# Softmax denominators folded with two half-width matmuls, a single transpose for the inverses, and moved pieces, in a routed attention followed by an MLP

## The chip, the core and the metric

The kernel runs on one core of a Trainium2 chip. The metric is the device time of one execution in microseconds (us); lower is better. A kernel is an instruction list for each of five engines: TensorE (PE in the profile, with its weight loads as PEld), VectorE (DVE), ScalarE (ACT), GpSimd (POOL) and SyncE (SP, which issues most transfers). Each list runs in the order in which the program emitted it; lists wait for one another by semaphores. A tile of PSUM is a bank, and a bank that is to be used again waits for its last readers.

## What is computed

The attention has 4 batches, 8 heads, 768 tokens and a head dimension of 64. Each query and key is assigned to the nearest of 16 centroids of its head, and a query attends only to keys of its own cluster. The result, seen as 3072 rows of 512, goes through a two-layer MLP with a PReLU.

```python
q_assign = np.argmax(np.einsum('bhsd,hcd->bhsc', q_n, c_n), axis=-1)
k_assign = np.argmax(np.einsum('bhsd,hcd->bhsc', k_n, c_n), axis=-1)
mask = q_assign[:, :, :, None] == k_assign[:, :, None, :]
scores = np.where(mask, scale * np.matmul(q, k.transpose(0, 1, 3, 2)), -1e9)
attn = np.exp(scores - np.max(scores, axis=-1, keepdims=True))
attn = attn / (np.sum(attn, axis=-1, keepdims=True) + 1e-09)
x = heads_to_columns(np.matmul(attn, v))          # 3072 x 512
h = x @ w_in                                      # 512 -> 2048
return (np.maximum(h, 0.0) + alpha * np.minimum(h, 0.0)) @ w_out
```

## The kernel before

**Units of work.** A pair n is two heads of a batch; there are 16. Pairs 0 to 11 (batches 0 to 2) are done in halves of 384 queries. For a half, all 6 chunks of 128 keys are scored against the queries (score, L712, with keys on the partitions), exponentiated by ACT, masked by DVE (mask, L761: E times "cluster of the query equals cluster of the key"; batch 0 gets its mask from a bf16 matmul, L740, instead), and multiplied by v on PE (weigh, L838). Pairs 12 to 15 (batch 3) are sorted by cluster beforehand, through a scratch in DRAM, so that a chunk of keys meets only the chunks of queries beside it. There the two halves are called sides, the product is weigh_near (L884), normalised results go to rows by PE transposes (to_rows, L923), are scattered by POOL (put_back, L933), and are read back and turned by DVE (fetch_back, L940).

**Denominators.** DVE adds the chunks of E (add_up L776, add_near L785), turns the sum in blocks of 32 by 32 (turn, L798) and reduces it (rows_sums, L805) to "part" of 128 x 24, 12 columns for each of the two heads. total (L813) folds it over the partitions by a matmul with a 0/1 matrix. invert (L821) takes reciprocals from PSUM, spreads them with one transpose for each head (64 partitions each, L832), and calls check (L326), which takes the smallest and largest bit pattern of the inverses by two reductions. normalise (L961) multiplies. The first half of batch 0 gets its denominators from PE (weigh with denominators, L854) instead. total, prep_sims, prep_clusters, order_sims, order_begins, one side of weigh_near and to_rows all take the one mps bank that misc (L84) hands out.

**MLP pieces.** While one batch half is attended, the MLP of the half before is fed in pieces (ffn_pieces, L972). hidden(f) makes block f of 16: four matmuls (eight PE records, since a float32 matmul is two records) into one of two fps banks that are used in turn, a copy gT by ACT, and the PReLU slope on gT by DVE in place (slopes, L978). Slopes of a block are emitted in the next hidden; where f % 4 is 3, directly after the copy (L997). final(i, f0) multiplies four blocks with w_out for 128 rows, again eight records, and when its sum over blocks is complete, ACT copies it to y or DVE adds it to y (L1015). For the first half of batch 0 the order is four hiddens, three finals, four hiddens, and so on; for all others eight hiddens, six finals, twice. Pieces also force the conversion of the float64 weights they need (convert, L242: split and join on DVE, scale on ACT, a product on POOL, L269).

**Order.** Everything is emitted by hand. There are 84 steps u, three to a pair's half (or sorted pair); s is a step's place among its three. Steps 0 to 11 attend the first half of batch 0, steps 12 to 23 its second. In these a step scores two chunks, weighs the two before, adds (from step 12), and in s = 2 turns and reduces; then come three slots with the pieces of the MLP and the preparations of later pairs, and total at the end of s = 2. Steps 12 to 23 are fed 3, 2, 2, 2, 2, 2, 3, 2, 2, 2, 2, 2 pieces: where it is two, they stand in the second and third slot. Thus hiddens 0 to 2 are in step 12, hidden 3 and the first final in 13, hiddens 4 and 5 in 15, 6 and 7 in 16, and the first final over blocks 4 to 7 in 17; hiddens 10 and 11 are in 19 and their first final in 20; hidden 15 and its final are in 23. A conversion that splits in a slot joins six slots later. From step 24 on a half or sorted pair scores three chunks, inverts and weighs the pair before, scores the other three, and spreads the DVE work (todo) over 12 slots: s = 0 has two of them, s = 1 and s = 2 five each. later (L95) puts a piece so many slots ahead; prep_at names a step and a slot; load_at a step. At the end the remaining pieces are fed at every second tick (L1228).

**Names that follow.** every is the bf16 image of all clusters of a pair (L433), copied by ACT from the mps bank of prep_clusters; order_counts (L553) finds the clusters of a pair that is to be sorted and counts them; order_blocks (L670) turns the sorted q and k; order_constants (L488) builds constants for the sort before step 25.

Of the kernel before, what the change touches and what calls it, by code (L numbers as in the profile page):

```python
# [10 lines left out]
FP32 = mybir.dt.float32  # L11
# [3 lines left out]
I32 = mybir.dt.int32  # L15
# [8 lines left out]
def kernel(  # L24
# [122 lines left out]
    alf = const.tile([NF, P], FP32, name="alf")  # L147
# [10 lines left out]
    fold = const.tile([P, P], FP32, name="fold")  # L158
    spread = const.tile([P, P // Q, P], BF16, name="spread")
    nc.gpsimd.memset(spread, 0.0)  # L160
    for g in range(P // Q):
        r = slice(g * Q, (g + 1) * Q)
        nc.gpsimd.tensor_copy(
            out=fold[r, :].rearrange("p (a i) -> p a i", i=Q),
            in_=ident[r, None, r].broadcast_to((Q, P // Q, Q)))
        nc.gpsimd.tensor_copy(out=spread[r, g, :], in_=fold[r, :])

# [34 lines left out]
    cn = const.tile([P, D], FP32, name="cn")  # L202
# [119 lines left out]
    lowest = const.tile([P, 2 * NP], FP32, name="lowest")  # L322
    highest = const.tile([P, 2 * NP], FP32, name="highest")
    WORDS = [float((127 + e) * 2 ** 23) for e in (-50, 40)]

    def check(n, half, inverses):  # L326
        i = 2 * n + half
        for to, op in ((lowest, ALU.min), (highest, ALU.max)):
            nc.vector.tensor_reduce(out=to[:, i:i + 1], in_=inverses.bitcast(I32), axis=AX.X,
                                    op=op)  # L330
# [157 lines left out]
    def order_constants():  # L488
        ordc = sorts["ordc"]
        stage = [ordc.tile([P, NX // PARTS, P], FP32, name=f"stage{i}") for i in range(STAGES)]  # L490
        for t in stage:
            nc.gpsimd.memset(t, 0.0)
        place = ordc.tile([P, HS], U16, name="place")
        nc.gpsimd.iota(place, pattern=[[1, HS]], base=0, channel_multiplier=0)

        number = ordc.tile([P, NX], I32, name="number")
        nc.gpsimd.iota(number, pattern=[[TS, NX]], base=0, channel_multiplier=1)

        kinds = [[[0, P // NC], [1, NC]], [[2, 2], [0, 2], [1, 2], [0, NC]],
                 [[0, 2], [1, 2], [0, Q]]]  # L500
        rows, cols = [], ordc.tile([P, 3], FP32, name="cols")
        brief = asg.tile([P, HS], FP32, name="simT")
        for i, pattern in enumerate(kinds):
            row = (ordc.tile([P, P], FP32, name=f"row{i}") if i else brief[:, 0:P])
            nc.gpsimd.iota(row, pattern=pattern, base=0, channel_multiplier=0,
                           allow_small_or_imprecise_dtypes=True)
            own = brief[:, P:2 * P]
            nc.gpsimd.tensor_tensor(out=own, in0=row, in1=ident, op=ALU.mult)
            nc.vector.tensor_reduce(out=cols[:, i:i + 1], in_=own, axis=AX.X, op=ALU.add)
            rows.append(row)  # L510
        same = brief[:, 2 * P:3 * P]
        nc.vector.tensor_scalar(out=same, in0=rows[1], scalar1=cols[:, 1:2], scalar2=None,
                                op0=ALU.is_equal)


        before, within = rows[1], rows[2]
        nc.vector.scalar_tensor_tensor(out=before, in0=rows[0], scalar=cols[:, 0:1],
                                       in1=same, op0=ALU.is_gt, op1=ALU.mult)
        nc.vector.scalar_tensor_tensor(out=same, in0=rows[0], scalar=cols[:, 0:1],
                                       in1=same, op0=ALU.is_equal, op1=ALU.mult)  # L520
        nc.vector.scalar_tensor_tensor(out=within, in0=rows[2], scalar=cols[:, 2:3],
                                       in1=same, op0=ALU.is_gt, op1=ALU.mult)
        nc.vector.tensor_tensor(out=within, in0=within, in1=before, op=ALU.add)


        shift = ordc.tile([P, 2], FP32, name="shift")
        nc.vector.tensor_scalar(out=shift[:, 0:1], in0=cols[:, 2:3], scalar1=-float(HS),
                                scalar2=None, op0=ALU.mult)
        nc.vector.tensor_scalar(out=shift[:, 1:2], in0=cols[:, 1:2], scalar1=2.0,
                                scalar2=float(S), op0=ALU.is_ge, op1=ALU.mult)  # L530
        nc.vector.tensor_scalar(out=shift[:, 1:2], in0=shift[:, 1:2], scalar1=-1.0,
                                scalar2=None, op0=ALU.add)
        begins = ordc.tile([P, NP - NO], FP32, name="begins")
        sorts.update(stage=stage, number=number, place=place, before=before, within=within,
                     shift=shift, begins=begins)
# [17 lines left out]
    def order_counts(n, ps):  # L553

        top, first, pieces = argmax(ps, exact=True)
        member = sorts["ordp"].tile([P, HS], BF16, name="mine")
        pieces.append(lambda: nc.vector.transpose(
            out=member, in_=top.rearrange("p t c -> p (t c)")))

        def scan():  # L560
            count = asg.tile([P, HS], FP32, name="simT")
            nc.vector.tensor_tensor_scan(count, member, member, 0.0, ALU.add, ALU.max)
            us[n] = member, count
        pieces.append(scan)
        for i, piece in enumerate(pieces):
            later(i, piece) if i else piece()
# [238 lines left out]
    def rows_sums(n, half):  # L805
        part = rdp.tile([P, 2 * NX], FP32, name="part")
        nc.vector.tensor_reduce(out=part, in_=accTs.pop((n, half)), axis=AX.X, op=ALU.add)
        parts[n, half] = part
# [4 lines left out]
    def total(n, half):  # L813

        if (n, half) in parts:
            ps = misc()
            nc.tensor.matmul(out=ps[:, 0:2 * NX], lhsT=fold, rhs=parts.pop((n, half)),
                             start=True, stop=True)
            totals[n, half] = ps

    def invert(n, half):  # L821

        if (n, half) not in totals:
            return
        ps = totals.pop((n, half))
        inv = rdp.tile([P, 2 * NX], FP32, name="inv")
        nc.vector.reciprocal(out=inv, in_=ps[:, 0:2 * NX])
        pool = sorts["ordp"] if n >= NO and half else rdp
        rd = pool.tile([P, HS], FP32, name="rd")
        for h in range(2):  # L830
            r = slice(h * D, (h + 1) * D)
            nc.vector.transpose(  # L832
                out=rd[r, :],
                in_=inv[r, h * NX:(h + 1) * NX, None].broadcast_to((D, NX, Q)))
        rds[n, half] = rd
        check(n, half, inv)

    def weigh(m, denominators=False):  # L838
# [24 lines left out]
        if denominators and done:  # L863
# [6 lines left out]
            inv = rdp.tile([P, 2 * NX], FP32, name="inv")  # L870
# [5 lines left out]
            for h in range(2):  # L876
                nc.vector.tensor_copy(out=inv[h * D + Q:(h + 1) * D, 0:NX],
                                      in_=inv[h * D:h * D + Q, 0:NX])
            rd = rdp.tile([P, HS], FP32, name="rd")
            nc.vector.transpose(out=rd, in_=inv[:, 0:NX, None].broadcast_to((P, NX, Q)))  # L880
            rds[n, half] = rd
            later(1, lambda: check(n, half, inv[:, 0:NX]))
# [17 lines left out]
    def normalise_near(n):  # L900
# [13 lines left out]

        starts = (4, 6) if n == NP - 1 else (6, 10)
# [7 lines left out]
    def to_rows(outT, rows, i):  # L923

        ps = misc()
        for j in range(HJ):
            nc.tensor.transpose(out=ps[:, j * P:(j + 1) * P],
                                in_=outT[:, (i * HJ + j) * P:(i * HJ + j + 1) * P],
                                identity=ident)
        later(1, lambda: nc.scalar.copy(  # L930
            rows[:, i * HJ:(i + 1) * HJ].rearrange("p j d -> p (j d)"), ps[:, 0:HS]))
# [40 lines left out]
    def ffn_pieces(b, half):  # L972
# [12 lines left out]
        def hidden(f):  # L985
# [11 lines left out]
            if f % FQ == FQ - 1:  # L997
                slopes()

        def final(i, f0, on, off):  # L1000
# [3 lines left out]
            unfinished[0] = not off  # L1004
            ps = pss[i]
# [41 lines left out]
    for (n, half), u in start_of.items():  # L1047
        def at(step, slot, piece):
            prep_at.setdefault((step, slot), []).append(piece)
        if half is None:  # L1050
# [7 lines left out]
            at(u - 4, FIRST, lambda n=n: prep_clusters(n))  # L1058
            for i in range(2):
                at(u - 2, FIRST + i, lambda n=n, i=i: order_blocks(n, i))  # L1060
                at(u - 1, FIRST + i, lambda n=n, i=i: order_queries(n, i))
            continue
        if half == 0:
# [16 lines left out]
            if n >= NCH:  # L1080
                at(u - 4, FIRST, lambda n=n: prep_clusters(n))
# [19 lines left out]
    def kept(block):  # L1101


        return {NS // UB - 2: 4, NS // UB - 1: 10}.get(block, 0)
# [52 lines left out]
    for u in range(TOGETHER, NS + 1):  # L1157
# [4 lines left out]
        if s == 0 or u == NS:  # L1162
# [6 lines left out]
            if prior[1] is None:  # L1169
                invert(prior[0], 1)  # L1170
# [21 lines left out]
            if half is None:  # L1192
# [4 lines left out]
                         lambda n=n: (total(n, 0), turn(n, 1), rows_sums(n, 1)),  # L1197
                         lambda n=n: invert(n, 0)]
                todo += [lambda: None] * 3 + [lambda n=n: total(n, 1)]
# [33 lines left out]
    good = const.tile([P, 2], FP32, name="good")  # L1233
    nc.vector.tensor_reduce(out=good[:, 0:1], in_=highest, axis=AX.X, op=ALU.max)
# [212 lines left out]
```

## Time and profile before

Three executions took 1002.57, 1004.88 and 1003.51 us, median 1003.51; the profiled one took 1003.53 with a span of 1001.4. TensorE's granted clock was full but for 7 us in all before 85 us.

| stretch, us | what | PE busy | DVE busy | POOL busy |
|---|---|---|---|---|
| 84.0 to 204.9 | batch 0, second half; MLP of the first | 119.8 of 120.9 | 94.5 | 26.1 |
| 204.9 to 302 | batch 1, with order_constants | 93.6 of 97.1 | 75.6 | 2.2 |
| 302 to 634 | batches 1 and 2 | 330.9 of 332.0 | 256.5 | 92.3 |
| 680.5 to 708.9 | pair 12 | 28.4 of 28.4 | 23.0 | 0 |
| 708.9 to 737.0 | pair 13 | 24.8 of 28.1 | 26.5 | 10.5 |
| 737.0 to 765.7 | pair 14 | 25.4 of 28.7 | 21.3 | 12.9 |
| 765.7 to 791.7 | pair 15 | 26.0 of 26.0 | 20.2 | 8.9 |
| 791.7 to 824.0 | end of pair 15, rows back | 30.1 of 32.3 | 7.3 | 16.4 |
| 824.0 to 1001.4 | MLP of batch 3 alone | 171.6 of 177.4 | 29.3 | 0 |

The table is the profile's busy time of each engine in each stretch. Busy time of PE contains the modelled end of each matmul: a hidden's record is busy 0.49 us, and the next one starts 0.32 us after it. A final's records start 0.43 us apart. In the page's groups, a line gives engine, operation, output and inputs, shape and count, then busy time in all and the mean of one in ns, then the idle time of the engine before such instructions and what ended it. In the timeline a line is one run of equal instructions: start, length, and in brackets the idle time before it with its releaser.

### The profile page before, as it was taken

Reading aid. Unit: us, or ns where it says so; the run is one execution under the profiler, and the core shown is the slowest. Engines: PE = TensorE matmul, PEld = TensorE weight load, DVE = VectorE, ACT = ScalarE, POOL = GpSimd, SP = SyncE. Lnnn points to the kernel's source line nnn. Section 1 sums busy time; section 2 is a strip of 40 time slices with the busy share of each in tenths; the row PEclk is TensorE's granted clock in tenths of the full one; section 3 lists DMA queues with packets and bytes.
Section 4 is the critical chain, followed back from the end, with each engine's and each line's share of the span. In section 5 each row is a group of like instructions: output and inputs, shape, how many; then the busy total and the mean of one; then the engine's idle time right before and its main releaser. Section 6 shows DMA issues by size and latency. Waiting matters only on the chain.

```text
span 1001.4 us, 10929 instructions
## 1 busy us (share of the span) xinstructions
PE 968.5 (97%) x3955; PEld 482.1 (48%) x3955; DVE 650.4 (65%) x1209; ACT 259.6 (26%) x468; POOL 211.8 (21%) x249
## 2 busy tenths in 40 slices
PE   8899999989999999999999999999988999999997
PEld 5434444445454454545445454454544545455453
DVE  5887788598487776877868698687987523021010
ACT  5655443223122221312222022231222101110110
POOL 2323222000000644301000263620044540000000
PEclk9989999999999999999999999999999999999999
DMA  6533553032100252415010121710521020000000
GB/s 248 199 108 108 137 135 71 16 67 44 32 1 21 87 114 56 84 40 106 1 32 0 53 80 34 148 35 17 85 60 31 24 50 22 0 5 29 0 1 34
DMA packets 174286, 60.46 MB, mean 60 GB/s; under 512 B 161216, under 2 KB 164752, under 8 KB 174224
## 3 DMA queue, kind: packets, MB, share of 16 engines
q1 hardware_dynamic: 168768, 51.42, 21.7%
q0 software_dynamic: 4608, 7.87, 2.3%
q8 instruction: 33, 0.54, 0.2%
q10 hardware_dynamic: 848, 0.39, 0.2%
q14 instruction: 29, 0.24, 0.1%
HBM read 45.15 MB, written 14.16 MB: 59 GB/s over the span
## 4 chain that ended last, share of the span: by engine, by line
PE 87%; DVE 8%; ACT 2%; issue 1%; DMA 1%; ACTq 0%; POOL 0%; DVEq 0%; POOLq 0%
PE fps L1007 31%; PE fps L989 31%; PE vps L861 8%; PE sps L731 7%; PE fps L731 3%; PE sps L740 1%; PE vps L897 1%; PE mps L371 1%; DVE gT L981 1%; DVE more L772 1%; PE mps L897 1%; DVE acc L801 1%; ACT E L752 1%; ACT member L416 1%; DMA aq<-member 1%
## 5 line engine op out<-in xcount | busy, mean ns | idle before, releaser
L989 PE MATMUL fps<-xT,w_in_sb 128*128 128x384 f32 x1024 | 342.9, 490 | 1.8 <-DVE y L1015 1.8
L1007 PE MATMUL fps<-w_out_sb,gT 128*128 128x512 f32 x768 | 339.2, 596 | 2.1 <-DVE gT L981 1.1
L989 PEld LDWEIGHTS fps<-xT,w_in_sb 128*128 128x128 f32 x1024 | 190.8, 190 | 140.5 <-issue 5.2
L1007 PEld LDWEIGHTS fps<-w_out_sb,gT 128*128 128x128 f32 x768 | 143.5, 190 | 173.9 <-issue 162.1
L637 POOL DMA_INDIRECT scratch<-stage,off x96 | 101.7, 1059 | 333.9 <-DMA stage<-in_v_dram 275.3
L981 DVE SCALAR_TENSOR_TENSOR gT<-gT,alpha 128x384 f32<-128x384 f32 x128 | 80.5, 635 | 133.8 <-ACT gT L995 127.1
L995 ACT COPY gT<-fps 128x384 f32<-128x384 f32 x128 | 61.3, 479 | 337.3 <-PE fps L989 328.4
L731 PE MATMUL sps<-qkT 64*128 64x384 f32 (+1 forms) x512 | 97.8, 501 | 0.7 <-ACT E L752 0.7
L772 DVE SCALAR_TENSOR_TENSOR more<-aq,key,more 128x384 f32<-128x384 bf16 (+1 forms) x136 | 74.5, 604 | 27.4 <-ACT more L752 14.0
L752 ACT ACTIVATE E<-sps 128x768 f32<-128x768 f32 (+1 forms) x81 | 61.2, 802 | 74.0 <-PE sps L740 45.8
L935 POOL DMA_INDIRECT back<-rows,place x48 | 48.7, 1015 | 108.9 <-ACT rows L930 95.2
L731 PEld LDWEIGHTS sps<-qkT 64*128 64x128 f32 x512 | 46.3, 189 | 45.2 <-issue 16.8
L861 PE MATMUL vps<-E,vt 128*64 128x384 f32 x356 | 67.0, 502 | 0.0
L1015 DVE TENSOR_TENSOR y<-y,fps 128x512 f32<-128x512 f32 x30 | 20.5, 683 | 67.3 <-PE fps L1007 67.3
L772 DVE SCALAR_TENSOR_TENSOR E<-aq,key,E 128x384 f32<-128x384 bf16 (+1 forms) x104 | 56.6, 601 | 8.3 <-ACT E L749 3.9
L782 DVE TENSOR_TENSOR acc<-acc,E 128x768 f32<-128x768 f32 x47 | 44.9, 955 | 16.7 <-ACT E L752 15.4
L1013 ACT COPY y<-fps 128x512 f32<-128x512 f32 x24 | 14.1, 586 | 140.3 <-PE fps L1007 127.4
L752 ACT ACTIVATE more<-sps 128x768 f32<-128x768 f32 (+1 forms) x47 | 35.5, 796 | 38.7 <-PE fps L1007 21.6
L861 PEld LDWEIGHTS vps<-E,vt 128*64 128x64 f32 x356 | 23.3, 138 | 32.4 <-issue 32.1
L861 PE MATMUL vps<-more,vt 128*64 128x384 f32 x220 | 38.8, 491 | 0.0
L269 POOL TENSOR_TENSOR w_in_sb<-w_in_sb,power 128x512 f32<-128x512 f32 x16 | 22.2, 1387 | 70.9 <-DVE w_in_sb L266 70.9
L269 POOL TENSOR_TENSOR w_out_sb<-w_out_sb,power 128x512 f32<-128x512 f32 x16 | 23.5, 1473 | 52.9 <-DVE w_out_sb L266 52.9
(175 smaller groups left out, 741.1 us busy)
## 6 DMA issues: line engine op xcount, KB each, us to landing
raw<-in_moe_w_in_dram SPq DMA_DIRECT2D x16, 512.0 KB
raw<-in_moe_w_out_dram SPq DMA_DIRECT2D x16, 512.0 KB
out_dram<-y SPq DMA_DIRECT2D x24, 256.0 KB
vt<-in_v_dram SPq DMA_DIRECT2D x12, 384.0 KB
qk<-in_q_dram SPq DMA_DIRECT2D x48, 96.0 KB
qk<-in_k_dram SPq DMA_DIRECT2D x48, 96.0 KB
qk<-scratch SPq DMA_DIRECT2D x32, 96.0 KB
qk<-in_q_dram SPq DMA_DIRECT2D x4, 384.0 KB
```

What stands on the lines that cost most here:

```text
L269: nc.gpsimd.tensor_tensor(out=dst, in0=dst, in1=power[0].bitcast(FP32), op=ALU.mult)
L637: nc.gpsimd.indirect_dma_start(out=scratch[n][1][h * NX + xx], out_offset=bass.IndirectOffsetOnAxis(ap=ranks[n][:, xx, h:h + 1], axis=0), ...
L731: nc.tensor.matmul(out=bank(ps, h, m), lhsT=qkT[r:r + D, S + c * P:S + (c + 1) * P], rhs=qkT[r:r + D, tokens], start=True, stop=not early_ ...
L752: nc.scalar.activation(out=E[:, :, 0:m], in_=ps[:, :, 0:m], func=AF.Exp, scale=SCALE)
L772: nc.vector.scalar_tensor_tensor(out=e, in0=of, scalar=keys[n][:, NJ + c, h:h + 1], in1=e, op0=ALU.is_equal, op1=ALU.mult)
L782: nc.vector.tensor_tensor(out=acc, in0=acc if first is None else first[3], in1=E, op=ALU.add)
L861: nc.tensor.matmul(out=po[r:r + D, 0:HS], lhsT=vts[n][:, h, c, :], rhs=e[:, h, :], start=(c == 0), stop=(c == NJ - 1))
L935: nc.gpsimd.indirect_dma_start(out=to[i], out_offset=bass.IndirectOffsetOnAxis(ap=place[:, h, j:j + 1], axis=0), in_=rows[:, j, h * D:(h + ...
L981: nc.vector.scalar_tensor_tensor(out=gs[f], in0=gs[f], scalar=alpha[:, f:f + 1], in1=gs[f], op0=ALU.mult, op1=ALU.max)
L989: nc.tensor.matmul(out=ps[:, 0:HS], lhsT=w_in_sb[:, c, f * P:(f + 1) * P], rhs=xTs[b, half][:, c, :], start=(c == 0), stop=(c == NCH - 1))
L995: nc.scalar.copy(gs[f], ps[:, 0:HS])
L1007: nc.tensor.matmul(out=ps[:, 0:DM], lhsT=gs[f][:, i * P:(i + 1) * P], rhs=w_out_sb[:, f, :], start=on and f == f0, stop=off and f == f0 + ...
```

## The change

- **Folding.** The matrix fold becomes two, folds, each with the columns of one head and zeros for the other. total takes two accumulating matmuls of 12 columns, so that a head's sums land on that head's own partitions. invert then has one reciprocal of 12 columns for a half, and one transpose over all 128 partitions (spread_out). For sorted pairs total and invert take both sides in one call at the end of the pair.
- **Checks.** Inverses of a batch stay in one tile; check_inverses reduces a whole batch by two instructions, when the first inverse of the next batch is made.
- **Slopes.** The flush after every fourth hidden goes; final flushes instead.
- **Rows.** to_rows takes an fps bank in place of mps, and its starts become 6 and 9 slots for all pairs (before 6 and 10, and 4 and 6 for the last).
- **Pieces moved.** The last two pieces of order_counts go two slots later. prep_clusters goes to slot 0 (before 2) for sorted pairs and for others from step 24 on. order_blocks goes from the slots 2 and 3 two steps ahead of its pair to the slots 0 and 1 one step ahead. order_constants leaves its DVE work to four pieces, 5 to 8 slots later. In the last block of steps 12 pieces (before 10) are kept for the end.
- **Tiles.** Several constants share a tile that is used later for something else; this makes room.

```diff
+    folds = const.tile([P, 2, P], FP32, name="folds")
+    nc.gpsimd.memset(folds, 0.0)
+    for h in range(2):
+        nc.gpsimd.tensor_copy(out=folds[:, h, h * D:(h + 1) * D],
+                              in_=fold[:, h * D:(h + 1) * D])
...
-            later(i, piece) if i else piece()
+            later(i if i < len(pieces) - 2 else i + 2, piece) if i else piece()
...
-    def total(n, half):
-        if (n, half) in parts:
-            ps = misc()
-            nc.tensor.matmul(out=ps[:, 0:2 * NX], lhsT=fold, rhs=parts.pop((n, half)),
-                             start=True, stop=True)
-            totals[n, half] = ps
+    def total(n, *halves):
+        if (n, halves[0]) in parts:
+            ps = totals[n, halves[0]] = misc()
+            for i, half in enumerate(halves):
+                part = parts.pop((n, half))
+                for h in range(2):
+                    nc.tensor.matmul(out=ps[:, i * NX:(i + 1) * NX], lhsT=folds[:, h, :],
+                                     rhs=part[:, h * NX:(h + 1) * NX],
+                                     start=(h == 0), stop=(h == 1))
...
-        for h in range(2):
-            r = slice(h * D, (h + 1) * D)
-            nc.vector.transpose(
-                out=rd[r, :],
-                in_=inv[r, h * NX:(h + 1) * NX, None].broadcast_to((D, NX, Q)))
-        check(n, half, inv)
+    def spread_out(n, half, inv):
...
+        nc.vector.transpose(out=rd, in_=inv[:, :, None].broadcast_to((P, NX, Q)))
...
-        starts = (4, 6) if n == NP - 1 else (6, 10)
+        starts = (6, 9)
...
-        ps = misc()
+        ps = ps_f.tile([P, 512], FP32, name="fps")
...
             fresh.append(f)
-            if f % FQ == FQ - 1:
-                slopes()
...
             unfinished[0] = not off
+            slopes()
...
-                at(u - 2, FIRST + i, lambda n=n, i=i: order_blocks(n, i))
+                at(u - 1, i, lambda n=n, i=i: order_blocks(n, i))
...
-        return {NS // UB - 2: 4, NS // UB - 1: 10}.get(block, 0)
+        return {NS // UB - 2: 4, NS // UB - 1: 12}.get(block, 0)
...
-                         lambda n=n: (total(n, 0), turn(n, 1), rows_sums(n, 1)),
-                         lambda n=n: invert(n, 0)]
-                todo += [lambda: None] * 3 + [lambda n=n: total(n, 1)]
+                         lambda n=n: (turn(n, 1), rows_sums(n, 1))]
+                todo += [lambda: None] * 4 + [lambda n=n: total(n, 0, 1)]
```

## The prediction

> **What bounds the kernel now.** I read the page's busy shares first, then what TensorE waited for, then the timeline around each wait. TensorE bounds:
>
> ```profile
> PE 968.5 (97%) x3955; PEld 482.1 (48%) x3955; DVE 650.4 (65%) x1209; ACT 259.6 (26%) x468; POOL 211.8 (21%) x249
> ```
>
> Only 33 us of the 1001.4 us span are idle on it: about 11 before 104 us, 6 at the tail, which the change doesn't touch, and some 16 in between. So DVE time saved is worth something only where a TensorE wait hangs on it, and any TensorE time added counts in full. The waits of TensorE (us in total, times, longest):
>
> ```profile
> PE mps L927 <- DVE inv L827: 4.2, 2, 2.7
> PE mps L817 <- DVE part L807: 3.9, 3, 1.7
> PE fps L989 <- DVE y L1015: 1.8, 1, 1.8
> PE mps L817 <- ACT every L433: 1.6, 3, 0.6
> PE fps L1007 <- DVE gT L981: 1.1, 2, 0.9
> ```
>
> L927 (to_rows) waits for the single mps bank, L817 (total) for sums or for that bank, L989 for an fps bank. Two pieces of the timeline price what is added. The first is a fold of two matmul records, then a matmul L572 of the same weights' shape with four:
>
> ```profile
> 265.57 0.30 PE L817 MATMUL mps<-part,fold 128*128 128x24 f32 x2
> 265.71 6.68 PE L1007 MATMUL fps<-w_out_sb,gT 128*128 128x512 f32 x15
> ...
> 316.03 0.50 PE L572 MATMUL mps<-simT,row 128*128 128x1 f32 x4
> 316.39 5.83 PE L1007 MATMUL fps<-w_out_sb,gT 128*128 128x512 f32 x13
> ```
>
> From start to the next line's start: 0.14 us for two records, 0.36 for four, although L572 is one column wide. The second piece is step 17 on DVE, with TensorE's final beside it:
>
> ```profile
> 133.79 2.17 DVE L981 SCALAR_TENSOR_TENSOR gT<-gT,alpha 128x384 f32<-128x384 f32 x2
> ...
> 135.47 7.13 PE L1007 MATMUL fps<-w_out_sb,gT 128*128 128x512 f32 x16
> ...
> 135.88 2.01 DVE L782 TENSOR_TENSOR acc<-acc,E 128x768 f32<-128x768 f32 x2
> ...
> 137.93 0.98 DVE L801 STREAM_TRANSPOSE acc<-acc 128x768 f32<-128x768 f32 x1
> 138.94 0.95 DVE L807 TENSOR_REDUCE part<-acc 128x24 f32<-128x768 f32 x1
> 139.81 0.97 DVE L354 STREAM_TRANSPOSE qkT<-qk 128x768 f32<-128x768 f32 x1
> 140.70 0.39 DVE L251 TENSOR_SCALAR power<-raw 128x512 uint32<-128x512 uint32 x1
> 141.00 0.42 DVE L253 TENSOR_SCALAR w_in_sb<-raw 128x512 uint32<-128x512 uint32 x1
> 141.34 0.69 DVE L263 SCALAR_TENSOR_TENSOR power<-raw,power 128x512 uint32<-128x512 uint32 x1
> 141.94 0.69 DVE L266 SCALAR_TENSOR_TENSOR w_in_sb<-raw,w_in_sb 128x512 f32<-128x512 uint32 x1
> 142.54 0.68 DVE L1015 TENSOR_TENSOR y<-y,fps 128x512 f32<-128x512 f32 x1
> ```
>
> The two L981 are the slopes of hidden blocks 6 and 7; both stand ahead of the sums. L1015 marks the place of this step's first final in DVE's queue.
>
> [...] the step's L1015 comes after everything emitted before it. [...] the four L572 records come 111 ns apart, so narrower operands save nothing. [...] a slope takes 0.61 us alone and 1.64 beside L269.
>
> **The change, part by part** (TensorE time). A wait costs its idle time plus about 0.2 us, since a matmul's busy time (0.49) outlasts the normal spacing (0.32).
>
> 1. *Folds.* Each of the 28 sums is folded by two matmuls of two records in place of one. By L572, (0.36 - 0.14) = 0.22 us each: 28 x 0.223 = **+6.2**. They stand in streams with no idle, so nothing hides them.
>
> 2. *Slopes.* A hidden no longer flushes its own slope when f % 4 is 3; the next final does. From the second batch half on, eight hiddens precede finals that start with blocks 0 to 3, so block 7 is read 6 us later: nothing lost. But batch 0's first half takes finals after every four hiddens, and each final reads the fourth block with its seventh record, 6 x 0.43 = 2.58 us after its start. Where the final is in a later slot, the slope is queued behind what DVE was given meanwhile.
>  Step 17 (block 7): the chain from the step's scores through exponentials, adds, turn, sums, transpose, split and join ends at 142.6 now. Without the second L981 the adds still wait for the exponentials, which end at 135.0 and 135.7, so it ends at about 141.9, and 0.6 for the slope gives 142.5. TensorE wants it at 135.47 + 2.58 = 138.05: +4.5.
>  Step 20 (block 11): the join ends at 174.2 now, 173.4 without the slope; slope to 174.0; wanted at 167.80 + 2.58 = 170.38: +3.7.
>  Step 13 (block 3): TensorE resumes at 103.09 now; a split (0.7) and a join (1.3) get ahead of the slope: 105.0, +1.9.
>  Step 23 (block 15): two transposes (1.4) and the keys (0.45) get ahead: about +1.5.
>  Sum **+11.6**. The stretch has 0.3 us of TensorE idle before step 23, so nothing absorbs it. Bounds: 0, if DVE were in time, and 15, with a slope beside L269 (1.64 in place of 0.61) in each.
>
> 3. *Rows in fps banks.* The waits of L927 for mps go: 2.68, 1.55, 1.25 and 0.95, with 0.2 each: **-7.3**. But the rows take a turn in the ring of two fps banks, so the hidden after them finds the bank of the hidden before, whose copy ends 0.49 + 0.48 = 1.0 us after its last record began, where 0.32 and the rows' own 0.33 have passed: with the restart 0.5 us. And since the rows' copy is issued one slot later, behind the next hidden's, the user of the rows' bank waits 1.2 us (the pair of copies at 802.53 and 802.91 shows it). Counted through the order of pieces, the eight groups of rows (two of them, in the last step's group, fall between finals of one block and cost nothing) give four short and four long waits: 6.7; if all eight are short, 4.0. Taken: **+5.4**; the ends are 0 and 6.7.
>
> 4. *One total for both sides, at the end of the step.* L817's wait for the first side at 752.80 goes: 1.75 + 0.2 = **-2.0**. The sums are in DVE's queue five slots ahead of the new place.
>
> 5. *Counting pieces two slots later, clusters in slot 0.* Waits at 296.06 and 598.40 (1.07 each) for sums behind L557 go: **-2.6**. The copies of every (0.62 three times, 0.33) get two slots more before total: **-2.9**. Order_blocks moves a step later, past total on DVE, and a reload that needs its buffer waits in SP's queue with it (12.9 us on L673 now, some 6 more); the readers move as far, so 0.
>
> 6. *Order_constants spread.* The DVE work from 216.3 to 220.3 delays L1015 and with it the hidden at 223.01: 1.85 + 0.2 = **-2.0**. The pieces return one by one some slots later, where sums have 1.5 us of room.
>
> 7. *DVE.* A sum's inverse costs 0.30 + 1.16 + 0.27 (reciprocal, two half transposes, checks); later 0.30 + 0.58. That is 0.85 us x 28, and 8 reductions replace 64: some 24 us of DVE, but under TensorE's stream: 0 beyond items 4 and 5. Constants at the start: one memset and two copies of GpSimd, estimated 0.8 us from its rows there, end before rank is read at 12.7: 0. Two pieces more are kept for the end: moved, not added.
>
> Sum: 6.2 + 11.6 + 5.4 - 7.3 - 2.0 - 2.6 - 2.9 - 2.0 = +6.4. The profiled execution took 1003.53 (span 1001.4), the median of the others 1003.51: **1009.9**.
>
> **The rivals.** (a) *Slopes in time*, faster: DVE reaches them before the seventh record, for instance because it no longer stands waiting for ScalarE's copy. It decides at 138.05 and 170.38; DVE's queue as shown speaks against it. 1009.9 - 11.6 = 998.3. (b) *Free banks*: the ring isn't as I read it and the rows never wait. 1009.9 - 5.4 = 1004.5. (c) *Waits come back*: where the sorted batch keeps DVE 90% busy (26.5 of 28.1 us from 708.9), removed waits return as waits for sums, so items 4 and 5's sums (4.6) give nothing: 1014.5. (d) *The change doesn't do what it says*: DVE's inverses stay on the path; nothing shows them there.
>
> **How the numbers follow.** Likeliest case 0.57 (1007 to 1013 by its own bounds), (a) 0.17, (b) 0.12, (c) with the upper bounds 0.14. A measurement can tell about 0.2%, 2 us, from no change. Then faster is (a), 0.17; within 0.2% is (b), 0.12; slower the rest, 0.71. Leaving (a) out with the upper part of (c) would drop more than 2 in 10, so the range runs from 998 to 1016.
>
> **What would show it.** DVE gT L981 heads TensorE's waits, with stretches of 4 us near 138 and 170; L817 has 112 records; L927 waits no more for mps, but L989 does for ACT rows or gT; the waits at 223, 296, 598 and 752 are gone. I am wrong if the first final after blocks 4 to 7 runs through without a gap.

## The result, and the profile after

The changed kernel takes 1019.23 us (median of four executions, 1017.43 to 1020.29), the kernel before 1003.04 (four, 1001.78 to 1004.88) on the same chip. The ratio is 1.0158, with a 95% interval of 1.0134 to 1.0182: slower by 16 us. The prediction was 1009.9, with a range that ended at 1016. The profiled execution of the changed kernel has a span of 1018.4 us at a mean TensorE clock of 0.989, against 1001.4 at 0.995 before.

The busy shares and the first two groups of the page of the changed kernel (line, engine, tiles, shapes, count, then busy time in all and ns of one, then idle time before and what ended it):

```profile
PE 983.6 (97%) x4011; PEld 491.3 (48%) x4011; DVE 625.5 (61%) x1119; ACT 259.6 (25%) x468; POOL 211.5 (21%) x252
...
L1037 PE MATMUL fps<-w_out_sb,gT 128*128 128x512 f32 x768 | 343.7, 601 | 12.8 <-DVE gT L1012 12.8
L1020 PE MATMUL fps<-xT,w_in_sb 128*128 128x384 f32 x1024 | 343.7, 491 | 2.7 <-ACT gT L1026 1.5
```

L1037 is final (L1007 before), L1020 hidden (L989), L1012 the slopes (L981). The busy time of TensorE is 983.6 us in place of 968.5. Taken from the spans, its idle time is 1018.4 - 983.6 = 34.8 us in place of 1001.4 - 968.5 = 32.9. So of the 17.0 us between the two spans **15.1 are busy time and only 1.9 idle time**. What TensorE waited for (us in total, times, longest) has changed its names all the same:

```profile
PE fps L1037 <- DVE gT L1012: 12.8, 5, 4.5
...
PE mps L929 <- issue: 1.6, 3, 1.0
PE fps L1020 <- ACT gT L1026: 1.5, 5, 0.6
PE fps L958 <- ACT gT L1026: 1.1, 2, 0.6
...
PE fps L1020 <- ACT y L1043: 0.7, 1, 0.7
```

The waits for an mps bank behind the inverses (4.2 us), for sums (3.9), for the copies of every (1.6) and for L1015 (1.8) are gone. A final that waits for slopes stands in their place.

The timeline of step 17, the place that the prediction worked out, in the changed kernel (start, length, engine, instruction, and in brackets the idle time before it with its releaser):

```profile
135.96 0.61 DVE L1012 SCALAR_TENSOR_TENSOR gT<-gT,alpha 128x384 f32<-128x384 f32 x1
...
137.18 2.40 DVE L811 TENSOR_TENSOR acc<-acc,E 128x768 f32<-128x768 f32 x2 [0.62 <-ACT E L781]
...
137.61 2.84 PE L1037 MATMUL fps<-w_out_sb,gT 128*128 128x512 f32 x6
...
144.23 0.61 DVE L1012 SCALAR_TENSOR_TENSOR gT<-gT,alpha 128x384 f32<-128x384 f32 x1
...
145.00 6.23 PE L1037 MATMUL fps<-w_out_sb,gT 128*128 128x512 f32 x10 [4.54 <-DVE gT L1012]
145.77 0.34 PEld L1037 LDWEIGHTS fps<-w_out_sb,gT 128*128 128x128 f32 x1 [0.51 <-issue]
146.63 0.34 PEld L1037 LDWEIGHTS fps<-w_out_sb,gT 128*128 128x128 f32 x1 [0.52 <-issue]
...
148.33 0.34 PEld L1037 LDWEIGHTS fps<-w_out_sb,gT 128*128 128x128 f32 x1 [0.52 <-issue]
148.91 0.19 PEld L1037 LDWEIGHTS fps<-w_out_sb,gT 128*128 128x128 f32 x1 [0.24 <-issue]
149.34 0.19 PEld L1037 LDWEIGHTS fps<-w_out_sb,gT 128*128 128x128 f32 x1 [0.24 <-issue]
```

The first slope (block 6) is done at 136.57. The second (block 7) is behind the adds, the turn, the sums, a transpose and a split, and is done at 144.84; the final stops after six of its records and goes on 0.16 us later. This is the gap that the prediction drew, 4.54 us long where it said 4.5. But then look at the weight loads, one for each record of the final. From 145.77 to 148.33 they start 0.86 us apart, from 148.91 on 0.43. **For some 3.4 us after the gap TensorE works at half its clock.** The windows view shows it in the steps 17, 20 and 23 (stretch, its length, busy time of PE, PEld, DVE, ACT and POOL, then the granted clock, the DMA share and GB/s):

```profile
core 0: us, PE busy (x) PEld busy (x) DVE busy (x) ACT busy (x) POOL busy (x), PEclk, DMA share, GB/s
141.00:152.00 11.00, 7.00 (x18) 3.39 (x20) 8.01 (x15) 0.00 (x0) 2.83 (x2) 0.84 0.81 114
179.00:190.00 11.00, 7.21 (x20) 3.41 (x20) 6.77 (x12) 0.00 (x0) 2.07 (x3) 0.84 0.00 0
216.00:228.00 12.00, 9.94 (x32) 4.20 (x30) 8.40 (x16) 2.49 (x4) 0.00 (x0) 0.72 0.42 77
```

11 x 0.16 + 11 x 0.16 + 12 x 0.28 = 6.9 us of full-speed time are missing there. The raw clock record of the trace says the same: one stretch at 0.5 of 3.413 us from 145.2, one from 182.8, and one twice as long from 220.3, 13.65 us in all, hence 6.8 lost. This is one execution: the mean clocks of the four are 0.989, 0.988, 0.992 and 0.991. By span times (1 - clock) they lose 8 to 12 us in all, 3 to 7 more than the kernel before in its profiled execution (5). Until its last 3 us the kernel before has only the two stretches near 50 and 70 us, which both kernels share.

So the busy time grew by 6.2 (the folds) and 6.8 (the clock), and some 2 us are left; the modelled ends of matmuls can shift time between busy and idle, so that these 2 us stay open.

### The profile page after: what moved, and what is told of

It is laid out like the page before. It is cut to its first block, busy times and chain, and to the rows that moved or that the text cites. A ratio compares the mean times of both kernels' runs of the same rounds, so it can differ in the third digit from the quotient of the medians.

```text
span 1018.4 us, 10958 instructions
## 1 busy us (share of the span) xinstructions
PE 983.6 (97%) x4011; PEld 491.3 (48%) x4011; DVE 625.5 (61%) x1119; ACT 259.6 (25%) x468; POOL 211.5 (21%) x252
## 4 chain that ended last, share of the span: by engine, by line
PE 90%; DVE 4%; ACT 2%; issue 1%; DMA 1%; POOL 0%; ACTq 0%; DVEq 0%; POOLq 0%
PE fps L1020 33%; PE fps L1037 32%; PE vps L896 8%; PE sps L760 8%; PE fps L760 3%; PE mps L850 1%; PE sps L769 1%; PE mps L387 1%; PE mps L929 1%; PE vps L929 1%; ACT E L781 1%; DVE acc L811 1%; DMA aq<-member 1%; ACT member L432 1%; ACT power L265 0%
## 5 line engine op out<-in xcount | busy, mean ns | idle before, releaser
L1037 PE MATMUL fps<-w_out_sb,gT 128*128 128x512 f32 x768 | 343.7, 601 | 12.8 <-DVE gT L1012 12.8
L1020 PE MATMUL fps<-xT,w_in_sb 128*128 128x384 f32 x1024 | 343.7, 491 | 2.7 <-ACT gT L1026 1.5
L1020 PEld LDWEIGHTS fps<-xT,w_in_sb 128*128 128x128 f32 x1024 | 190.7, 190 | 142.8 <-issue 4.9
L1037 PEld LDWEIGHTS fps<-w_out_sb,gT 128*128 128x128 f32 x768 | 144.2, 192 | 187.0 <-issue 179.0
L666 POOL DMA_INDIRECT scratch<-stage,off x96 | 99.1, 1033 | 329.0 <-DMA stage<-in_v_dram 271.7
L1012 DVE SCALAR_TENSOR_TENSOR gT<-gT,alpha 128x384 f32<-128x384 f32 x128 | 77.9, 610 | 121.2 <-ACT gT L1026 115.7
L760 PE MATMUL sps<-qkT 64*128 64x384 f32 (+1 forms) x512 | 100.0, 507 | 0.6 <-ACT E L781 0.6
L896 PEld LDWEIGHTS vps<-E,vt 128*64 128x64 f32 x356 | 23.4, 139 | 33.2 <-issue 32.6
L760 PE MATMUL fps<-qkT 64*128 64x384 f32 x160 | 36.2, 518 | 0.1
```

The lines of the kernel that those rows point to most:

```text
L666: nc.gpsimd.indirect_dma_start(out=scratch[n][1][h * NX + xx], out_offset=bass.IndirectOffsetOnAxis(ap=ranks[n][:, xx, h:h + 1], axis=0), ...
L760: nc.tensor.matmul(out=bank(ps, h, m), lhsT=qkT[r:r + D, S + c * P:S + (c + 1) * P], rhs=qkT[r:r + D, tokens], start=True, stop=not early_ ...
L896: nc.tensor.matmul(out=po[r:r + D, 0:HS], lhsT=vts[n][:, h, c, :], rhs=e[:, h, :], start=(c == 0), stop=(c == NJ - 1))
L1012: nc.vector.scalar_tensor_tensor(out=gs[f], in0=gs[f], scalar=alpha[:, f:f + 1], in1=gs[f], op0=ALU.mult, op1=ALU.max)
L1020: nc.tensor.matmul(out=ps[:, 0:HS], lhsT=w_in_sb[:, c, f * P:(f + 1) * P], rhs=xTs[b, half][:, c, :], start=(c == 0), stop=(c == NCH - 1))
L1037: nc.tensor.matmul(out=ps[:, 0:DM], lhsT=gs[f][:, i * P:(i + 1) * P], rhs=w_out_sb[:, f, :], start=on and f == f0, stop=off and f == f0 + ...
```

## The experiments

All are compared with the kernel before on the same chip: for E1 to E4 it took 1002.01 us, for E5 to E8 1004.3, for E9 and E10 1004.8. Ratios are to that, with 95% intervals.

**E1: the changed kernel with the slopes in time.** The flush after every fourth block comes back.

```diff
             fresh.append(f)
+            if f % FQ == FQ - 1:
+                slopes()
```

> The changed kernel with the old flush of slopes back in hidden (the flush in final stays, and finds nothing to do in the first batch). Theory, gaps and clock: the late slopes cost 11.6 us of TensorE gaps, and these cost four windows of 3.4 us at half clock, 6.8 us; without both the time is 1019.2 - 18.4 = 1000.8. Rival, gaps alone: the half-speed windows come from something else and stay: 1007.6. Rival, folds and banks: the slopes are a small part: above 1012.

Measured: 1003.55 us, ratio 1.0023 (1.0015 to 1.0031). Against the changed kernel's 1.0158 the flush is worth 0.0135, or 13.5 us, between the two expectations. No stretch at half clock is left but the first two: the mean clock is 0.995, as in the kernel before, and the clock from 141 to 152 us is 1.00 (0.84 in the changed kernel). But waits for sums are back, as the list of TensorE's waits and the timeline show:

```profile
PE mps L850 <- DVE part L837: 3.5, 4, 1.9
```

```profile
753.61 1.98 PE L1039 MATMUL fps<-w_out_sb,gT 128*128 128x512 f32 x4 [0.85 <-DVE gT L1012]
755.43 0.51 PE L850 MATMUL mps<-part,folds 128*128 128x12 f32 x4
757.80 0.61 PE L850 MATMUL mps<-part,folds 128*128 128x12 f32 x4 [1.86 <-DVE part L837]
```

L850 is total. The two waits of 1.07 us near 296 and 598 are shortened to 0.61 each, not removed, and the one at 752.80 of the kernel before has moved to 757.80 and grown to 1.86. This one hangs on the sorted rows that are read back. DVE turns them (L957 before, L988 here) ahead of the sums. The kernel before comes to this turn without a wait; E1, whose scores of pair 14 come 4.3 us earlier, stands there until the rows land, at nearly the same time:

```profile
746.14 1.03 DVE L957 STREAM_TRANSPOSE xT<-qk 128x384 f32<-128x384 f32 x2
```

```profile
745.98 1.04 DVE L988 STREAM_TRANSPOSE xT<-qk 128x384 f32<-128x384 f32 x2 [5.15 <-DMA qk<-back]
```

In E1's chain the transfers (2.9 us), this turn, the adds and the sums lead to total at 757.80 without a gap. So waits come back, as rival (c) of the prediction said, in the kernel in which DVE isn't late with slopes, but not for (c)'s reason: DVE isn't full there, it stands idle for 5.15 us.

**E2: the kernel before with late slopes alone**, and **E3: the same with TensorE kept busy in the gaps.** E3 puts 10, 19, 16 and 5 extra matmuls of the identity into the mps bank, ahead of the fourth block of the four first finals; nothing reads their result.

```diff
-            if f % FQ == FQ - 1:
-                slopes()
...
             unfinished[0] = not off
+            slopes()
...
+                if f == f0 + FQ - 1 and fill:
+                    idle = misc()
+                    for _ in range(fill):
+                        nc.tensor.matmul(out=idle[:, 0:P], lhsT=ident, rhs=ident,
+                                         start=True, stop=True)
```

> The kernel before with the late slopes alone. Gaps and clock: 1003 + 11.6 + 6.8 = 1021.4, with half-speed windows after the gaps of steps 17, 20 and 23. Gaps alone: 1014.6, clock as before.

> As e2_late, with idle matmuls of the identity (10, 19, 16 and 5 of them, into the mps bank, read by nobody) issued ahead of the fourth block of the first final after each group of four hiddens, so that TensorE works while it waits. Gaps and clock: the waits stay and the clock does not fall: 1014.6, up to 1017 where the fill outlasts a wait. Gaps alone: the same as e2_late or more.

Measured: E2 1014.6 us, ratio 1.0126 (1.0109 to 1.0143); E3 1011.19, ratio 1.0096 (1.0076 to 1.0116). E2's total is that of "gaps alone". It would have misled without its trace: the same group of matmuls (the scores of a step) is 15.4 us later than in the kernel before by step 24, which is the gaps and two stretches at half clock, and then some 3.7 us come back, of which 1.31 are the wait for sums at 296 and 1.31 the one at 598. Later each of the two has one more stretch at half clock, from 742.21 in E2 (mean clock 0.991) and from 767.69 in E3 (0.993). E3 shows the clock apart from the wait. The stretch from 141 to 152 in the windows view, E2 and then E3:

```profile
141.00:152.00 11.00, 6.92 (x16) 3.33 (x18) 8.11 (x15) 0.00 (x0) 2.84 (x2) 0.84 0.60 120
```

```profile
141.00:152.00 11.00, 10.73 (x63) 7.03 (x63) 9.65 (x17) 0.00 (x1) 2.85 (x2) 1.00 0.58 118
```

And E3's timeline there:

```profile
138.50 2.31 PE L1012 MATMUL fps<-w_out_sb,gT 128*128 128x512 f32 x5
140.65 4.41 PE L1010 MATMUL mps<-ident 128*128 128x128 f32 x38
145.32 4.53 PE L1012 MATMUL fps<-w_out_sb,gT 128*128 128x512 f32 x10 [0.27 <-DVE gT L981]
149.69 0.30 PE L817 MATMUL mps<-part,fold 128*128 128x24 f32 x2
```

The final still goes on at 145 because the slope comes no earlier, but its ten records then take 4.53 us at full clock. The step gains 1.6 us and step 20 gains 1.4; in medians E3 is 3.4 us below E2, and each of its four executions (1010.04 to 1013.37) is below each of E2's (1013.68 to 1014.9). More work on TensorE made the kernel faster.

**E4: the kernel before with the two half-width folds and the single transpose.**

```diff
-            nc.tensor.matmul(out=ps[:, 0:2 * NX], lhsT=fold, rhs=parts.pop((n, half)),
-                             start=True, stop=True)
+            part = parts.pop((n, half))
+            for h in range(2):
+                nc.tensor.matmul(out=ps[:, 0:NX], lhsT=folds[:, h, :],
+                                 rhs=part[:, h * NX:(h + 1) * NX],
+                                 start=(h == 0), stop=(h == 1))
```

> The kernel before with two half-width fold matmuls and one transpose for each half or side, all else as before (checks of each inverse, each side's total in its place). Theory: 28 x 0.22 = 6.2 us more on TensorE, of which DVE's relief (0.57 us for each) gives back the part of the waits for sums that it reaches: 1006 to 1009.5. Rival: DVE's relief pays for it: 1003 or less.

Measured: 1006.04 us, ratio 1.0045 (1.003 to 1.0059). In the timeline the fold of four records takes 0.37 us to the next start, where that of two took 0.14:

```profile
266.21 0.51 PE L826 MATMUL mps<-part,folds 128*128 128x12 f32 x4
266.58 7.11 PE L1013 MATMUL fps<-w_out_sb,gT 128*128 128x512 f32 x16
```

Every half moves the steps behind it by 0.22 us in E4, in E1 and in the changed kernel alike. The page's busy time of PE is 974.5, 6.0 above before.

**E5: the changed kernel with slopes in time in batch 0's first half only.** **E6: E5 with the fold of before** (one matmul, two half transposes). **E7: E6 with the rows' copy issued at once**, not a slot later.

```diff
+            if (b, half) == (0, 0) and f % FQ == FQ - 1:
+                slopes()
```

> The changed kernel with the old flush of slopes in the first half of batch 0 alone; later blocks keep the late flush. Theory: there the early flush makes DVE stand and wait for ScalarE's copy, and in e1_early that left waits for sums at 294, 598, 679 and 758 and for a slope at 754 (4.4 us of idle in all, none of them in the changed kernel). So 1003.5 - 4.4 = 999 where before takes 1002. Rival: these waits come from the earlier arrival of TensorE and stay: 1003.5.

> As e5_early_first, with the fold of before: one matmul of 24 columns for each half or side, two half transposes for the inverses, the rest of the change kept. Theory: 28 x 0.22 = 6.2 us less than e5: 993. Rival: the single transpose is what frees DVE for the sums, so that waits for sums return: 996 or more.

> As e6_one_fold, with ScalarE's copy of the rows emitted in to_rows itself and not one slot later. Theory: the long waits for a bank of rows come from the copy standing behind the next hidden's copy; four of them (1.6 us of idle, with 0.2 each 2.4 us) shrink: 2 us less than e6. Rival: ScalarE then stands still for the transposes and delays the hidden's copies: the same.

Measured: E5 1002.74 us, ratio 0.9988 (0.9974 to 1.0002); E6 998.88, ratio 0.9949 (0.9933 to 0.9966); E7 999.79, ratio 0.9953 (0.9937 to 0.997). E5's step 17 on TensorE:

```profile
135.43 7.13 PE L1039 MATMUL fps<-w_out_sb,gT 128*128 128x512 f32 x16
142.40 0.51 PE L850 MATMUL mps<-part,folds 128*128 128x12 f32 x4
```

This one condition, true in the first half alone, takes the kernel from 1.0158 to 0.9988: 0.0170, or 17 us. E5 is below E1 by 0.0035 (0.0013 to 0.0057 from the ends of the intervals), so late slopes are a gain in the later halves, where eight blocks precede a final; no wait for sums of 0.2 us or more is left in E5's trace. They aren't always in time there either, as E9 shows. E5 to E6 prices the folds by removal: 0.0039, 3.9 us. E6 is faster than both kernels. E7's earlier copy shortens the waits of 0.57 us for the rows' bank to 0.24, and the time stays the same; its profile has a new pause of 4.25 us at 733.48, of which more below.

**E8: the kernel before with the rows in fps banks, its rows at 6 and 9 slots and 12 pieces kept**, and **E10: with the bank alone.**

```diff
-        starts = (4, 6) if n == NP - 1 else (6, 10)
+        starts = (6, 9)
...
-        ps = misc()
+        ps = ps_f.tile([P, 512], FP32, name="fps")
...
-        return {NS // UB - 2: 4, NS // UB - 1: 10}.get(block, 0)
+        return {NS // UB - 2: 4, NS // UB - 1: 12}.get(block, 0)
```

E10 has only the second of these three.

> The kernel before with the rows alone changed: fps banks, starts 6 and 9, 12 pieces kept. Prediction's item 3: 7.3 us of waits for mps go, 5.4 come: 1.9 us less than before, 1000.1. Rival: total for the first side keeps its place in the middle of the step, and TensorE, which arrives earlier, waits there for sums instead: 1002.

> The kernel before with one word changed: the rows' transposes take a fps bank instead of an mps bank; starts of the rows and pieces kept back stay as they were. The prediction's item 3 gives waits of 7.3 us away (730.15, 758.25, 799.37, 803.44) and about 5 us of waits of later pieces for the fps bank, so a ratio of 0.998. If the 7.7 us that the earlier kernel with rows in fps lost came from the bank itself, this one loses the same, 1.007. If they came from the other two edits in it (rows one or two slots earlier or later, two more pieces kept back), which moved the pieces so that the total of a side came up before its partial sums were ready (2.41 and 3.29 us, each with a window at half clock behind it), this one has neither these waits nor the windows and stands within 0.3% of before.

Measured: E8 1012.01 us, ratio 1.0072 (1.0056 to 1.0089), which no expectation had; E10 1003.86, ratio 0.9995 (0.9987 to 1.0004). E8's timeline, and its windows view of the same place:

```profile
777.29 0.55 PE L927 MATMUL fps<-ident,qk 128*128 128x128 f32 x3
777.68 3.60 PE L1007 MATMUL fps<-w_out_sb,gT 128*128 128x512 f32 x8
784.57 0.59 PE L817 MATMUL mps<-part,fold 128*128 128x24 f32 x2 [3.29 <-DVE part L807]
```

```profile
781.00:788.00 7.00, 3.71 (x9) 2.13 (x9) 6.72 (x10) 0.00 (x0) 4.89 (x5) 0.76 0.07 24
```

Two pieces of work fewer stand ahead of a side's total there, so total comes up before its sums and waits 3.29 us. At 753.53 a hidden (2.85 us) stands ahead of it where the kernel before has a final (3.60), which is longer, and it waits 2.41 us (1.75 before). A stretch at half clock follows each: the mean clock is 0.91 from 740 to 760 us and 0.94 from 760 to 790. Which of the two small edits does it isn't separated. E10 has neither of these waits: its longest wait for sums is 1.2 us. Its profile has one stretch at half clock all the same, from 740.11, behind a pause of 1.50 us that is taken up at the end: eight records of weigh_near take 2.40 us there, from 740.69, where the same eight take 1.30 in E9, from 731.49. The bank alone is worth nothing that can be measured: the waits for mps go, and 0.24 to 0.57 us for a fps bank in many places come.

**E9: E6 with the rows back in mps.**

> This is the kernel with before's fold and with slopes in time in the first half (median 998.9 on an earlier chip whose kernel before took 1004.3), with the rows' transposes put back into the mps bank, all else the same. The prediction's item 3 says that the move costs TensorE 5.4 us in waits of pieces for a fps bank and takes 7.3 us of waits for a mps bank: back in mps the pieces' waits near 713 to 797 us (3.8 us together in the trace) go and L926's waits for an mps bank come, up to 7.3 us, so the ratio to before rises by 0.002 to 0.0035, to about 0.997 to 0.9985. The rival: with the total of both sides formed once, late, the mps bank is no longer held by a total that waits for the inverses, so that mps was free all along and the move of the rows alone cost its 3.8 us; then this kernel is the fastest, about 0.991.

Measured: 996.92 us, ratio 0.9934 (0.9914 to 0.9955); the interval overlaps that of E6. The waits of E9 for banks and slopes:

```profile
PE fps L1036 <- DVE gT L1009: 3.6, 3, 2.4
...
PE mps L955 <- ACT rows L958: 1.9, 2, 1.0
...
PE mps L440 <- ACT rows L958: 0.9, 1, 0.9
```

The waits for an mps bank behind the inverses don't come back; the total of both sides is formed late here. What comes is 2.8 us behind the rows' own copies. The longest wait for a slope, 2.4 us at 753.73, is in pair 14, where DVE has stood for the rows that are read back, and a stretch at half clock follows from 754.91 (eight records of a final take 5.23 us from 755.19, and 3.60 at full clock in the kernel before, from 747.46): in this trace a late slope costs time in a later half too. The move of the rows is no gain beside the merged totals. E6, E7 and E9 are faster than the kernel before, by 0.5 to 0.7%, and so than the changed kernel too.

## Why the prediction was wrong

The direction and the places of the gaps were right, and the size was not: 15.9 us (1.0158 x 1003.5) in place of 6.4. Two steps of the sum failed.

**The first step that failed is item 2, which left out the clock.** It counted the gaps: "Sum +11.6". Measured, the five waits for slopes are 12.8 us, less the 1.1 that the kernel before has: 11.7. What it left out is the clock, which is at half for 3.413, 3.413 and 6.827 us behind the gaps of the steps 17, 20 and 23: 6.8 us lost in the trace of the changed kernel. The half clock of step 17 is gone where the gap is filled (E3, clock 1.00 from 141 to 152), and these stretches are absent where the slopes are in time (E1 and E5, mean clocks 0.995 and 0.996). The whole of item 2 in the first half is 17 us by E5, against 11.6; in the two profiles the same scores are 18.9 us apart behind step 23. The last part, the later halves, was put at "nothing lost"; E1 against E5 shows a gain of some 3.5 us there. Item 2's upper bound of 15 came from a slope beside L269 (three that start during L269 take 1.62 to 1.64 us, the others about 0.61) and didn't contain the clock at all, though the profile of the kernel before shows 7 us at half clock before 85 us, right behind waits of 3.0 and 1.7 us. How much idle time stood ahead of such stretches is in the last section.

**The second is the credit for waits taken away, items 3 to 6: -11.4 together.** E6 has these parts without the folds, and slopes in time in the first half: -5.1 us (-6.7 to -3.4), the gain of late slopes in the later halves included. The folds cost some 2 us less than priced. Together that is 6.4 + 5.4 + 6.3 - 2 = 16.1, against 15.9.

The traces show where the credit is missing. The same scores are 19.4 us later in the changed kernel than before at 209 us (the kernel before's time), 16.5 at 709, and the end is 17.0 later. With 18 and then 6 folds of 0.22 us taken off, it gains 6.9 us up to 709, where 6.7 were priced (items 5 and 6 but for the wait at 734). Behind 709 it gains 0.9, where 4.7 were priced (items 3 and 4 and that wait). From the first scores of one sorted pair to those of the next, in us:

| kernel | pair 13 to 14 | 14 to 15 | sum |
|---|---|---|---|
| before | 28.1 | 28.7 | 56.8 |
| changed | 24.3 | 32.3 | 56.6 |
| E1 | 24.3 | 32.6 | 57.0 |
| E5 | 24.3 | 32.7 | 57.0 |
| E6 | 23.9 | 32.4 | 56.2 |
| E7 | 22.9 | 35.5 | 58.3 |
| E8 | 24.8 | 35.0 | 59.8 |
| E9 | 24.1 | 34.2 | 58.3 |
| E10 | 26.2 | 31.6 | 57.8 |

What pair 13 gains, pair 14 gives back, each time. The form differs: waits for sums in E1 and E8, pauses in the changed kernel, E5, E6, E7 and E10 (last section), a wait for a slope in E9. The prediction took each wait in these pairs as if nothing stood behind it. The rows that are read back are a candidate for what does: from the first scores of pair 13 to DVE's turn of these rows pass 37.3 us in the kernel before and 36.0 in the changed kernel, 37.6 in E1, 36.0 in E6 and 36.5 in E9, though pair 13 is some 4 us shorter in these four. No run changes that chain alone, so that it is the limit is not shown.

**Item 1, folds, +6.2:** 0.22 us each, exactly, and 28 of them on TensorE. In time E4 gives 4.5 us (3.0 to 5.9 from its interval) and E6 3.9 by removal. Item 7 put DVE's relief at nothing; the difference of about 2 us may be that relief, but no run has it by itself.

**Item 3, rows, +5.4 - 7.3:** the idle waits for the rows' banks in the changed kernel sum to 3.8 us, which is 5.6 with 0.2 for each of the nine: as predicted. But neither sum shows in the time: E10 has the bank change at 0.9995, E6 against E9 at +0.0015 with overlapping intervals. The -1.9 is not to be seen.

**Items 4 to 6, -9.5:** the named waits at 223, 296, 598 and 752 and those for every are all gone in the changed kernel. E9, which holds these parts with the fold of before, stands at -6.6 us (-8.6 to -4.5), some of it from late slopes in the later halves. Item 4's words "five slots ahead" left out what DVE may have to wait for ahead of the sums: E1 has the wait for sums at 757.80. That the changed kernel has none there is no merit of its order. It pauses between 755 and 757.5 anyway, for 1.6 us in three pieces, at L929 (weigh_near), which waits for nothing that the profile shows.

**What rivals had right:** (c), waits that come back as waits for sums, holds in E1, and in E8 in a worse form; in the changed kernel itself the time comes back as pauses. Its ground, a DVE that is busy (26.5 of 28.1 us are 94%, not 90%), is not what E1 shows. (a) and (b) are out: the gaps came, and the rows waited.

## What to carry to other kernels

An engine that applies something to another's operand must do so in its own queue before the long work, not "just before it is needed": here "just before" meant behind everything emitted meanwhile, and the slope of block 7 was done at 144.84, 8.3 us after that of block 6. That holds where the reader is near; where it came many us later, in the later halves, the late slopes were a gain (some 3.5 us, E1 against E5). Where gaps of TensorE are priced, look at the granted clock next to every gap before the sum is made: here the gaps of 4.54 and 3.79 us were each followed by 3.413 us at half clock, which loses 1.7 us, and gaps of 2.37 us (step 13) and 2.68 us (kernel before, 730.15) were followed by none. A wait taken away is worth its length only where nothing else stands behind it: here 4 us gained in one pair were given back in the next. Moving work between queues is judged with all parts in place: here the rows' bank was worth 0 alone and cost 7 us together with two small shifts of the pieces around it.

## What the runs showed of the hardware that was not expected

**How much idle time stands ahead of half clock.** The stretches at half clock in one trace start at whole multiples of 3.413 us from each other: from 49.65 on, the changed kernel's starts are 6, 22, 11, 11 and 233 multiples apart (49.65, 70.13, 145.22, 182.77, 220.31 and the tail, 1015.62), those of the kernel before 6 and 272 (49.79, 70.27 and 998.70). If the two traces are cut into windows of 3.413 us on that grid, from 6 us to 985, each of the 5 windows at full clock in which TensorE was idle for 1.92 us or more is followed by half clock, and none of the 8 that were idle for 0.9 to 1.4 us. Between lie 7 windows, of 1.55 to 1.85 us, 2 of them followed by half clock. Idle time alone doesn't decide there: the kernel before has two windows with 1.75 us of it, one from 66.86, with half clock behind it, and one from 749.53, without. In the first TensorE's matmuls are narrow (L731 with 64 rows, L740 with 32, L854 with 32 columns), in the second they are full (L1007, 128 by 128); whether that matters was not tried. So 1.92 us idle in a window of 3.413 was enough in these two traces, and what a gap cost went with how the grid cut it. The kernel before has a gap of 2.68 us at 730.15, cut into 1.57 and 1.11, and no stretch at half clock. The twice as long stretch from 220.31 follows two waits of 0.86 and 1.20 us, 1.76 of them in one window; in E2 the same two waits are followed by none, and the eight score records behind them take 1.56 us where they take 2.93 in the changed kernel. Why the changed kernel's second window stays at half speed although TensorE is busy for all of the 6.83 us from 220.31 isn't settled.

**Pauses without a releaser.** Where pair 13 gets faster, pair 14 gives most of it back: between the same scores the changed kernel gains 3.8 us and then loses 2.7, E6 gains 4.2 and loses 3.3, E7 gains 5.3 and loses 6.8. In each, ScalarE stands before an exponential or a copy while TensorE and DVE run dry. In the changed kernel:

```profile
757.40 1.54 SPq L978 DMA_DIRECT2D qk<-back  x4
...
757.47 0.49 ACT L778 ACTIVATE more<-fps 128x384 f32<-128x384 f32 x1 [0.94 <-remote]
```

ScalarE goes on 0.07 us after SyncE issued the transfers that read the rows back; in E7 it is 732.95 after 732.83, in E6 734.79 after 734.71, in E10 741.21 after 741.12. SyncE's issue itself comes 2.9 to 3.1 us after the start of the last of GpSimd's twelve scatters (754.53 in the changed kernel), so the pause may as well end with these. Whether one has to do with the other was not tried, and what ScalarE waits for there stays open.
